# Transposing phi(k) and the attention output by DMA in a TensorE-bound attention + MLP kernel

## The chip, the cores, the metric

One core of one Trainium2 chip. The metric is the device time of one execution in microseconds (us), the median of several runs.

## The reference, cut to what matters

```python
xn = layernorm(x)                                  # x: 2048 x 1024
out = x + A(xn) + B(xn)

# A: 32 heads of 32, four segments of 512 tokens, one after the other
q, k, v = xn @ wq, xn @ wk, xn @ wv
phi(t) = where(t > 0, t + 1, exp(t))
for s in range(4):
    a_dot = softmax(q_s k_s^T * scale + mask) @ v_s          # inside the segment
    a_mem = (phi(q_s) @ M) / (phi(q_s) @ z + 1e-6)           # memory of earlier segments
    o_s   = g * a_mem + (1 - g) * a_dot
    M += phi(k_s)^T @ v_s ;  z += sum of phi(k_s)
A = o @ wo

# B: MLP over tokens: hidden 3584
B = (gelu(layernorm(xn)^T @ w1 + b1) @ w2 + b2)^T
```

The output of the memory update for the last segment is never used, so phi(k) is needed for three of the four segments only.

## The kernel before

After the norm and the first MLP product, the attention runs in 32 *units*: unit `u` is segment `s = u // 8` and group `g = u % 8` of four heads. The second MLP product and the product with `wo` (*main* matmuls below) are emitted in slices between the pieces of a unit, so that TensorE has work while ScalarE, VectorE and GpSimd make the softmax weights. `LEAD = 2`: the projections of q and k are made two units ahead.

Operands lie in SBUF; matmuls write into PSUM, which this kernel uses as banks 0 to 7. A result is *evacuated* when ScalarE or VectorE copies it from its bank to SBUF. Both operands that have to be transposed go through TensorE with an identity matrix, into PSUM, and back:

```python
def proj_k(self, u, b):                       # k^T of one unit: 128 (4 heads x 32) x 512 tokens
    ...  # 8 matmuls into bank b
    fw.op("dve", lambda e: e.tensor_copy(self.kT[k][:], self.bank(b)), ...)

def k_transpose(self, u, b):                  # tokens to the partitions, for M += phi(k)^T v
    bb = self.bank_bf(b)[:, 0:512]
    with fw.group(reads=[self.R_kT[k], self.R_ident], writes=[self.R_bank[b]]):
        for c in range(4):
            fw.tp(bb[:, c * P:(c + 1) * P], self.kT[k][:, c * P:(c + 1) * P], self.ident[:])
    fw.op("act", lambda e: e.activation(self.etmp[1][:], bb, ACT.Exp), ...)
    self.phi(self.pk[j][:]..., self.R_pk[j], bb, self.R_bank[b], 1)    # DVE: min, then add + max

def o_transpose(self, u, b):                  # output of a unit, for the product with wo
    ...  # four tp of o_s into bank b, then:
    fw.op("act", lambda e: e.activation(self.oT[s % 2][:, g, :], bb, ACT.Copy), ...)

def proj_v(self, m, c, b):
    ...  # 8 matmuls into bank b
    fw.op("dve", lambda e: e.tensor_copy(self.vA[i][:, c, :, 0:D_HEAD], ...), ...)

for u in range(N_UNIT):
    n = 28 if s == 0 else 36                  # main matmuls in this unit
    n0, n1, n2 = (10, 8, 6) if s == 0 else (11, 9, 9)
    n3 = n - n0 - n1 - n2
    self.logits(u, 0)                         # banks 0-3, then one Exp on ACT
    if u: self.combine(u - 1)                 # DVE: o_s of the unit before
    self.main_emit(n0)
    self.logits(u, 1); self.main_emit(n1)
    self.logits(u, 2); self.main_emit(n2)
    self.weigh(u, 0); self.weigh(u, 1)
    self.proj_q(un, 0)                        # un = u + 2
    if u: self.o_transpose(u - 1, 2)
    if ...: self.k_transpose(u + 1, 3)        # not for segment 3
    self.weigh(u, 2)
    self.proj_k(un, 1)
    self.weigh(u, 3)                          # the last one also updates M with pk
    if ...: self.proj_v(m, u % 4, 2)
    self.main_emit(n3)
```

A helper (`FW`) puts the semaphore waits in. One of its rules matters here: two engines that read the same PSUM bank wait for each other, so readers of one bank run one after the other.

The softmax here doesn't subtract the row's maximum and nothing guards it: scores larger than these inputs give would overflow.

## Time and profile before

| | kernel before |
|---|---|
| median | 758.41 us (fast runs 757.46 to 758.64) |
| profiled span | 756.9 us, clock 0.999 |
| TensorE (PE) busy | 717.7 us, 95% |
| one unit, segment 0 / segment 1 | 14.48 / 16.57 us |

The unit lengths are distances between the first logits matmuls of one unit and the next in the timeline of TensorE (means of units 1 to 6, and 9 to 14).

The page of the kernel before: busy time of each engine with its share of the span, and shares of the chain that ended last.

```profile
PE 717.7 (95%) x5058; PEld 338.3 (45%) x5154; DVE 277.2 (37%) x617; ACT 280.4 (37%) x301; POOL 112.3 (15%) x154
...
PE 92%; DVE 4%; issue 2%; SPq 1%; DMA 1%; ACT 0%; DVEq 0%; another core or an unknown queue 0%
```

The table of stretches of the same kernel; the columns are named in its head.

```profile
core 0: us, PE busy (x) PEld busy (x) DVE busy (x) ACT busy (x) POOL busy (x), PEclk, DMA share, GB/s
...
350.00:420.00 70.00, 68.56 (x565) 33.01 (x574) 35.74 (x79) 29.16 (x32) 10.90 (x16) 1.00 0.34 72
420.00:490.00 70.00, 68.59 (x539) 32.28 (x547) 36.92 (x79) 28.95 (x29) 11.21 (x16) 1.00 0.35 74
```

In the attention part TensorE has 68.6 us of work in every 70 us; VectorE and ScalarE are half as busy. So a microsecond counts only if it is one of TensorE's.

What the transposes cost on TensorE is read from *starts*. The timeline of the kernel before (start, duration, engine, line, operation, count), inside one unit of segment 1 (unit 14):

```profile
463.16 1.89 PE L188 MATMUL ps_all<-xnT_70,wq_666 128*128 128x512 bf16 x8
464.88 0.39 PE L194 MATMUL ps_all<-ident,o_s_1739 128*128 128x128 bf16 x4
465.10 0.39 PE L194 MATMUL ps_all<-ident,kT_1727 128*128 128x128 bf16 x4
465.33 0.46 PE L188 MATMUL ps_all<-vA_64,pT 128*128 128x33 bf16 x12
```

The records say 0.39 us for each group of four, but they overlap: the next group starts 0.22 us later, and the work after it 0.23 us later. A group of four transposes is worth about 0.22 us, not 0.39.

The same timeline where attention starts (in brackets the idle time before it, and what ended it):

```profile
237.57 0.39 PE L194 MATMUL ps_all<-ident,kT_1727 128*128 128x128 bf16 x4
239.70 0.40 PE L188 MATMUL ps_all<-qT_1724,kT_1727 32*128 32x512 bf16 x4 [1.74 <-DVE pk_1733 L673]
```

The first k transpose lies in bank 0, which the first logits need; TensorE waits until phi has read it.

### The profile page before, as it was taken

The numbers are of one execution on the slowest core, as the hardware profiler recorded it, in microseconds if no ns is written. First come the engines' busy times: TensorE is split into PE (matmuls) and PEld (weight loads), VectorE is DVE, ScalarE is ACT, GpSimd is POOL, SyncE is SP. The second block draws the span as 40 slices with busy tenths as digits, with TensorE's granted clock in tenths as the row PEclk, the third lists the DMA queues.
The fourth block names the chain that finished last, engine by engine and source line by source line (L and its number), as shares of the span: only waits on it lengthen the run. The fifth ranks groups of instructions, "written<-read, shape, count | busy, mean of one in ns | idle before, by whom it ended". The sixth has DMA issues, their size and how long they took to land.

```text
span 756.9 us, 11693 instructions
## 1 busy us (share of the span) xinstructions
PE 717.7 (95%) x5058; PEld 338.3 (45%) x5154; DVE 277.2 (37%) x617; ACT 280.4 (37%) x301; POOL 112.3 (15%) x154
## 2 busy tenths in 40 slices
PE   0999999999998999999999999999999999999996
PEld 0544444444443444444444444444444444444442
DVE  6920000000002343344444555544455553444443
ACT  2781212121213434435444434444443444343430
POOL 3630000000000111111121111112111111211220
PEclk9999999999999999999999999999999999999999
DMA  9439224225307161461542506054250615415003
GB/s 255 136 100 218 72 56 112 55 59 133 49 25 194 29 132 52 83 132 34 100 90 44 120 15 133 31 102 91 42 119 15 132 33 101 102 33 105 15 5 121
DMA packets 164604, 65.79 MB, mean 87 GB/s; under 512 B 125642, under 2 KB 156362, under 8 KB 164554
## 3 DMA queue, kind: packets, MB, share of 16 engines
q1 hardware_dynamic: 164554, 65.04, 36.8%
q8 instruction: 41, 0.67, 0.4%
q14 instruction: 9, 0.07, 0.0%
HBM read 59.79 MB, written 5.24 MB: 86 GB/s over the span
## 4 chain that ended last, share of the span: by engine, by line
PE 92%; DVE 4%; issue 2%; SPq 1%; DMA 1%; ACT 0%; DVEq 0%; another core or an unknown queue 0%
PE ps_all L188 90%; PE ps_all L194 2%; DVE ln_st L575 1%; SPq L210 1%; DVE ln_st L574 1%; DMA brow_51<-in_B_b_dram 1%; DVE ln_mv L576 0%; DVE xn_tmp_76 L607 0%; DVE ln_rs L584 0%; DVE fin_8202 L966 0%; DVE fin_8203 L966 0%; ACT xn_tmp_75 L604 0%; DVE xn_tmp_74 L607 0%; DVE ln_rs L585 0%; ACT xnT_70 L622 0%
## 5 line engine op out<-in xcount | busy, mean ns | idle before, releaser
L743 ACT ACTIVATE pT<-ps_all 128x1536 bf16<-128x1536 f32 (+1 forms) x96 | 152.9, 1593 | 201.6 <-PE ps_all L188 201.6
L749 POOL TENSOR_SCALAR_AFFINE_SELECT pT<-pT 128x512 bf16<-128x512 bf16 x128 | 86.9, 691 | 599.5 <-ACT pT L743 599.5
L662 ACT ACTIVATE gT<-ps_all,b1c 128x512 bf16<-128x512 f32 x56 | 37.8, 689 | 134.5 <-PE ps_all L188 134.5
L710 DVE CAST vA_63<-ps_all 128x512 bf16<-128x512 f32 x16 | 11.1, 694 | 187.9 <-PE ps_all L188 187.7
L188 PE MATMUL ps_all<-h,w1s_79 128*128 128x512 bf16 x311 | 72.9, 385 | 2.7 <-issue 2.2
L188 PE MATMUL ps_all<-h,w1s_80 128*128 128x512 bf16 x314 | 72.4, 381 | 0.3
L188 PE MATMUL ps_all<-h,w1s_81 128*128 128x512 bf16 x251 | 55.6, 379 | 0.3
L188 PE MATMUL ps_all<-gT,w2h_671 128*128 128x512 bf16 x213 | 53.0, 380 | 2.8 <-PE ps_all L188 0.9
L188 PE MATMUL ps_all<-gT,w2h_673 128*128 128x512 bf16 x214 | 53.1, 380 | 2.6 <-PE ps_all L188 1.1
L188 PE MATMUL ps_all<-gT,w2h_670 128*128 128x512 bf16 x219 | 53.6, 381 | 0.3
L188 PE MATMUL ps_all<-gT,w2h_672 128*128 128x512 bf16 x218 | 53.3, 381 | 0.4 <-PE ps_all L188 0.2
L783 DVE CAST ost_1736<-ps_all 128x264 bf16<-128x264 f32 (+1 forms) x64 | 23.7, 391 | 79.6 <-PE ps_all L188 79.6
L783 DVE CAST ost_1737<-ps_all 128x264 bf16<-128x264 f32 (+1 forms) x64 | 23.7, 392 | 74.7 <-PE ps_all L188 74.7
L188 PEld LDWEIGHTS ps_all<-h,w1s_80 128*128 128x128 bf16 x320 | 31.5, 98 | 38.4 <-issue 1.1
L188 PEld LDWEIGHTS ps_all<-h,w1s_79 128*128 128x128 bf16 x320 | 30.9, 99 | 37.1 <-issue 3.6
L188 PEld LDWEIGHTS ps_all<-h,w1s_81 128*128 128x128 bf16 x256 | 25.0, 98 | 30.2
L188 PE MATMUL ps_all<-wo_sb,oT_1744 128*128 128x512 bf16 x126 | 32.6, 380 | 1.4 <-remote 0.3
L188 PEld LDWEIGHTS ps_all<-gT,w2h_671 128*128 128x128 bf16 x224 | 19.4, 97 | 30.8 <-PE ps_all L188 6.9
L188 PEld LDWEIGHTS ps_all<-gT,w2h_673 128*128 128x128 bf16 x224 | 19.4, 97 | 30.8 <-PE ps_all L188 6.9
L188 PE MATMUL ps_all<-wo_sb,xnT_68 128*128 128x512 bf16 x127 | 30.6, 380 | 1.2 <-ACT xnT_68 L835 0.7
L188 PEld LDWEIGHTS ps_all<-gT,w2h_672 128*128 128x128 bf16 x224 | 19.3, 98 | 25.3 <-issue 3.6
L188 PEld LDWEIGHTS ps_all<-gT,w2h_670 128*128 128x128 bf16 x224 | 19.3, 98 | 25.3 <-issue 3.6
(167 smaller groups left out, 870.9 us busy)
## 6 DMA issues: line engine op xcount, KB each, us to landing
w1s_79<-in_B_w_dram SPq DMA_DIRECT2D x5, 1024.0 KB, 5.5
w1s_80<-in_B_w_dram SPq DMA_DIRECT2D x5, 1024.0 KB, 6.1
w1s_81<-in_B_w_dram SPq DMA_DIRECT2D x4, 1024.0 KB, 5.7
wq_666<-in_A_wq_dram SPq DMA_DIRECT2D x16, 256.0 KB, 3.2
wq_667<-in_A_wq_dram SPq DMA_DIRECT2D x16, 256.0 KB, 7.2
wk_668<-in_A_wk_dram SPq DMA_DIRECT2D x16, 256.0 KB, 2.9
wk_669<-in_A_wk_dram SPq DMA_DIRECT2D x16, 256.0 KB, 4.9
w2h_670<-in_B_w_dram SPq DMA_DIRECT2D x8, 448.0 KB, 4.8
```

Source lines behind the costliest of these rows:

```text
L188: ins = self.nc.tensor.matmul(*args, **kwargs)
L194: ins = self.nc.tensor.transpose(out, in_, ident)
L210: ins = es.eng.dma_start(out_ap, in_ap)
L574: fw.op("dve", lambda e: e.bn_stats(st[:, 0:6], src[:, 0:512]), reads=[self.R_xin[c]], writes=[R])
L575: fw.op("dve", lambda e: e.bn_stats(st[:, 6:12], src[:, 512:1024]), reads=[self.R_xin[c], R], writes=[R])
L662: fw.op("act", lambda e: e.activation(self.gT[:, fc, half * 512:(half + 1) * 512], self.bank(b), ACT.Gelu_apprx_tanh, bias=self.b1c[:, fc: ...
L710: fw.op("dve", lambda e: e.tensor_copy(self.vA[i][:, c, :, 0:D_HEAD], self.bank(b).rearrange("p (h d) -> p h d", d=D_HEAD)), reads=[self.R ...
L743: fw.op("act", lambda e: e.activation(self.pT[:, :, off:off + total], self.ps[:, 0:4, 0:total], ACT.Exp, scale=SCALE), reads=self.R_bank[0:4],
L749: fw.op("pool", lambda e: e.affine_select(d, d, pattern=[[0, 4], [1, P]], compare_op=ALU.is_ge, fill=0.0, base=0, channel_multiplier=-1), ...
L783: fw.op("dve", lambda e: e.tensor_copy(dst, self.ps[:, b, 0:n * VW]), reads=[self.R_bank[b]], writes=[self.R_ost[o][qb]])
```

## The change

The intent is to take 55 of the transposes (24 of phi(k), 31 of the output) off TensorE and let the DMA engines do them from SBUF to SBUF. phi(k) is now computed before the transpose, straight after the K projection: Exp reads the projection's bank. The first of k's transposes is issued straight after the projections of unit 0, no longer after those of unit 1. ScalarE, which loses the copies of the output, takes V's evacuation. V's product moves ahead of K's, and the fill counts `n0, n1, n2` change, so that more main matmuls stand between K's product and the next logits.

```diff
-        ins = es.eng.dma_start(out_ap, in_ap)
+        ins = es.eng.dma_start(out_ap, in_ap, transpose=True) if transpose else es.eng.dma_start(out_ap, in_ap)
...
 def proj_k
         fw.op("dve", lambda e: e.tensor_copy(self.kT[k][:], self.bank(b)), ...)
+        if u // N_GRP < N_SEG - 1:
+            fw.op("act", lambda e: e.activation(self.etmp[1][:], self.bank(b), ACT.Exp),
+                  reads=[self.R_bank[b]], writes=[self.R_etmp[1]])
+            self.phi(self.mtmp[1][:], self.R_mtmp[1], self.kT[k][:], self.R_kT[k], 1)
 def proj_v
-        fw.op("dve", lambda e: e.tensor_copy(self.vA[i]..., self.bank(b)...
+        fw.op("act", lambda e: e.activation(self.vA[i]..., self.bank(b)..., ACT.Copy),
-    def k_transpose(self, u, b):            # four tp, Exp, phi
...
+    def k_transpose(self, u):
+        j = u % 2
+        self.fw.dma(self.pk[j][:], self.mtmp[1][:], reads=[self.R_mtmp[1]], writes=[self.R_pk[j]], transpose=True)
+    def o_transpose_dma(self, u):
+        self.fw.dma(self.oT[s % 2][:, g, :]..., self.o_s[o][:]..., ..., transpose=True)
 loop over units
-            n0, n1, n2 = (10, 8, 6) if s == 0 else (11, 9, 9)
+            n0, n1, n2 = (9, 7, 6) if s == 0 else (10, 8, 8)
             self.logits(u, 2)
+            if u + 1 < N_UNIT and (u + 1) // N_GRP < N_SEG - 1:
+                self.k_transpose(u + 1)
+            if u:
+                self.o_transpose_dma(u - 1)
             self.main_emit(n2)
 ...
-            if u:
-                self.o_transpose(u - 1, 2)
-            if u + 1 < N_UNIT and (u + 1) // N_GRP < N_SEG - 1:
-                self.k_transpose(u + 1, 3)
             self.weigh(u, 2)
-            if un < N_UNIT:
-                self.proj_k(un, 1)
-            self.weigh(u, 3)
             m = u // 4 + 1
             if m < 2 * N_SEG:
                 self.proj_v(m, u % 4, 2)
+            self.weigh(u, 3)
+            if un < N_UNIT:
+                self.proj_k(un, 1)
             self.main_emit(n3)
```

The last output transpose, in the tail, stays on TensorE.

More of the change, by code (lines that the diff above doesn't have):

```diff
@@ L199, in dma @@
     def dma(self, out_ap, in_ap, reads=(), writes=(), is_output=False, issuer="sp", extra=(),
-            record_reads=True):
+            record_reads=True, transpose=False):
         es = self.E[issuer]
@@ L709, in proj_v @@
                       self.wv_sb[:, dc, bv * 512:(bv + 1) * 512], start=(dc == 0), stop=(dc == N_DCH - 1))
-        fw.op("dve", lambda e: e.tensor_copy(self.vA[i][:, c, :, 0:D_HEAD],
-                                             self.bank(b).rearrange("p (h d) -> p h d", d=D_HEAD)),
+        fw.op("act", lambda e: e.activation(self.vA[i][:, c, :, 0:D_HEAD],
+                                            self.bank(b).rearrange("p (h d) -> p h d", d=D_HEAD), ACT.Copy),
               reads=[self.R_bank[b]], writes=[self.R_vA[i][c]])
-    def k_transpose(self, u, b):
-        fw = self.fw
-        k, j = u % 3, u % 2
-        bb = self.bank_bf(b)[:, 0:512]
-        with fw.group(reads=[self.R_kT[k], self.R_ident], writes=[self.R_bank[b]]):
-            for c in range(4):
-                fw.tp(bb[:, c * P:(c + 1) * P], self.kT[k][:, c * P:(c + 1) * P], self.ident[:])
-        fw.op("act", lambda e: e.activation(self.etmp[1][:], bb, ACT.Exp),
-              reads=[self.R_bank[b]], writes=[self.R_etmp[1]])
-        self.phi(self.pk[j][:].rearrange("p c d -> p (c d)"), self.R_pk[j], bb, self.R_bank[b], 1)
+    def k_transpose(self, u):
+        j = u % 2
+        self.fw.dma(self.pk[j][:], self.mtmp[1][:], reads=[self.R_mtmp[1]], writes=[self.R_pk[j]], transpose=True)
     LOGIT_STEPS = [[0], [1], [2, 3]]
@@ L826, in combine @@
               reads=[self.R_prod], writes=[R_os])
+    def o_transpose_dma(self, u):
+        s, g, o = u // N_GRP, u % N_GRP, u % 2
+        self.fw.dma(self.oT[s % 2][:, g, :].rearrange("p (q t) -> p q t", q=4),
+                    self.o_s[o][:].rearrange("p q j -> p (q j)"),
+                    reads=[self.R_os[o]], writes=[self.R_oT[s % 2][g]], transpose=True)
     def o_transpose(self, u, b):
@@ L900, in attention_and_out @@
             self.proj_k(u, 6 + u)
-        self.k_transpose(0, 0)
+            if u == 0:
+                self.k_transpose(0)
         for u in range(N_UNIT):
```

## The prediction

> **What bounds the kernel.** TensorE. On the page PE is 95% busy and the chain that ended last is 92% PE. In the stretches table each 70 us between 280 and 700 us holds 68.4 to 69.0 us of PE work at full clock; DVE is about 50% busy, ACT 41%, DMA 0.34 to 0.42. Only what changes PE's own stream, or makes it wait, counts.
>
> **Removed from PE.** 31 transposes of the attention output and 24 of k, four 128x128 matmuls each. In the timeline of one unit (16.53 us) they start at 464.88 and 465.10, the next work at 465.33: 0.225 us per group, all on the critical path. 55 x 0.225 = 12.4 us. Other matmuls only change order.
>
> **Start of attention.** The timeline shows PE idle 1.74 us at 238 us, until phi(k) of unit 0 releases bank 0. That goes, but Exp of the second k now precedes the first logits Exp on ACT: net -1 us.
>
> **Moved.** V's cast (694 ns x28) leaves DVE; on ACT it replaces the copy of the output transposes (603 ns x31). Neither engine bounds: no direct gain. A unit now ends with K projection, main matmuls, next logits, which need K's bank. Its readers run one after the other (kT cast 0.68, Exp 0.6), about 1.4 us with hand-over. In segments 1 to 3 ten main matmuls (2.2 us) cover that; in segment 0 only six (1.3 us, counted from slightly earlier): 0.3 x 8 = +2.4 us. Shorter fill before the second logits, and waits for DMA semaphores: +1.
>
> **The DMA transposes.** 55 of 128 KB on the SP queue, up to two per unit. k's has about 10 us before the next DVE phi overwrites its source; the output's about 9 us before fused matmuls need it, and only in a segment's first unit. The Trainium skill (VectorE: DVE Perf Modes, "The three transpose paths") gives 1309 ns for a 128x128 DMA transpose; my estimate from it is at most 4 x 1.3 = 5.2 us, likelier 3, as fixed latency is not paid four times. Loads of 256 KB land in 3 to 7 us here (DMA table). Then nothing waits, and DMA's share rises from 0.37 to about 0.5. No trace here shows a DMA transpose: the weak point.
>
> **Sum.** 758.6 - 12.4 - 1 + 2.4 + 1 = 748.6; freed DVE may give a little back: 748 us, range 744 to 762. Faster by over 2% (below 743.5) 0.07, within 2% 0.77, slower 0.16.
>
> **What would show each step right.** In attention PE transposes only in the tail (4); a unit with both transposes 16.1 instead of 16.53 us in segments 1 and 2; in segment 0 about 14.3 instead of 14.45, with small PE gaps before its first logits, ended by ACT's Exp of k; the gap at 238 us gone; transposes landing in 2 to 6 us; no wait of PE on one; little DVE wait for the k product's buffer.
>
> **What would make it wrong.** Transposes that take 8 us or more each, or keep the SP queue or all DMA engines busy: then DVE stalls on the k product's buffer, everything behind it comes late, weight loads queued behind them land late, and PE waits in every unit; 24 units times several us would be slower by over 2%. If transposes took 2 us and segment 0's gap did not appear, the time would be 744 to 745.

## The result, and the profile after

The changed kernel took 747.72 us (747.44 to 748.58), against 758.41 us. The ratio is 0.9865, 95% interval 0.9846 to 0.9884. Ratios here and below are the mean time of one kernel's runs over that of the other's of the same rounds, so they are not quite the ratio of the medians. Executions over 1.5% slower than the fastest of the same kernel are left out of the means.

The page of the changed kernel, the same two lines:

```profile
PE 706.4 (95%) x4842; PEld 326.3 (44%) x4934; DVE 260.0 (35%) x585; ACT 286.6 (38%) x302; POOL 113.9 (15%) x154
...
PE 89%; DVE 5%; issue 2%; ACT 2%; SPq 1%; DMA 1%; DVEq 0%; ACTq 0%
```

The stretches of the changed kernel:

```profile
350.00:420.00 70.00, 68.40 (x516) 31.03 (x523) 34.96 (x75) 30.72 (x30) 11.48 (x17) 1.00 0.42 92
420.00:490.00 70.00, 68.45 (x532) 31.40 (x540) 33.65 (x72) 31.15 (x30) 13.60 (x20) 1.00 0.49 105
```

TensorE is still the limit, with the same density of work; DMA's share rose from about 0.35 to 0.42 to 0.49 here. The timeline of the same unit 14 in the changed kernel shows nothing between the Q projection and the products with V:

```profile
456.86 1.89 PE L188 MATMUL ps_all<-xnT_70,wq_666 128*128 128x512 bf16 x8
458.58 0.46 PE L188 MATMUL ps_all<-vA_64,pT 128*128 128x33 bf16 x12
458.89 0.22 PE L188 MATMUL ps_all<-MZbf,pqT_1732 128*128 128x132 bf16 x1
458.94 1.89 PE L188 MATMUL ps_all<-wv_sb,xnT_70 128*128 128x512 bf16 x8
```

The start of attention in the changed kernel (TensorE and ScalarE): the wait of 1.74 us is gone, but a new one of 1.04 us follows. Exp of the second k (L703) runs first on ScalarE, so the Exp of the first logits (L740) starts only at 238.06, and the next logits need the banks that it reads.

```profile
236.50 0.40 PE L188 MATMUL ps_all<-qT_1724,kT_1727 32*128 32x512 bf16 x4
236.83 2.12 PE L188 MATMUL ps_all<-gT,w2h_670 128*128 128x512 bf16 x9
237.57 0.60 ACT L703 ACTIVATE etmp_1741<-ps_all 128x512 bf16<-128x512 f32 x1 [1.26 <-DVE kT_1728 L700]
238.06 1.87 ACT L740 ACTIVATE pT<-ps_all 128x2048 bf16<-128x2048 f32 x1
239.99 0.34 PE L188 MATMUL ps_all<-qT_1724,kT_1727 32*128 32x384 bf16 x4 [1.04 <-ACT pT L740]
```

At the end of each unit of segment 0 the first logits of the next unit are late. This is the timeline of TensorE, VectorE and ScalarE at the end of unit 1 in the changed kernel (lines of other instructions left out):

```profile
263.12 1.67 PE L188 MATMUL ps_all<-xnT_68,wk_669 128*128 128x512 bf16 x7
...
264.63 1.46 PE L188 MATMUL ps_all<-gT,w2h_671 128*128 128x512 bf16 x6
264.83 0.69 DVE L700 CAST kT_1727<-ps_all 128x512 bf16<-128x512 f32 x1 [0.90 <-PE ps_all L188]
265.61 0.60 ACT L703 ACTIVATE etmp_1741<-ps_all 128x512 bf16<-128x512 f32 x1 [2.55 <-DVE kT_1727 L700]
...
266.35 0.40 PE L188 MATMUL ps_all<-qT_1726,kT_1729 32*128 32x512 bf16 x4 [0.27 <-ACT etmp_1741 L703]
```

Cast, then Exp, then the bank is free: 1.4 us from 264.83 to 266.2, and only six main matmuls to cover it. The gap of 0.27 us is there eight times, before the first logits of units 1 to 8.

The transposes in the DMA table of the changed kernel (tiles, issuing queue, count, median us from issue to landing; the output goes to `oT` in segments 0 and 2, to `xnT_68` in 1 and 3):

```profile
pk_1733<-mtmp_1743 SPq DMA_TRANSPOSE x12, 2.4
pk_1734<-mtmp_1743 SPq DMA_TRANSPOSE x12, 6.0
oT_1744<-o_s_1738 SPq DMA_TRANSPOSE x8, 2.3
oT_1744<-o_s_1739 SPq DMA_TRANSPOSE x8, 3.8
xnT_68<-o_s_1738 SPq DMA_TRANSPOSE x8, 2.3
xnT_68<-o_s_1739 SPq DMA_TRANSPOSE x7, 2.8
```

Where the 10.80 us between the two profiled spans lie, from starts in the two timelines of TensorE:

| stretch | before | after | difference |
|---|---|---|---|
| up to the first Q projection | 230.66 | 229.50 | -1.16 |
| Q projection to the first logits | 9.04 | 7.00 | -2.04 |
| unit 0 | 14.29 | 15.52 | +1.23 |
| units 1 to 7 (segment 0) | 101.33 | 100.58 | -0.75 |
| units 8 to 22 | 248.69 | 242.05 | -6.64 |
| units 23 to 30 | 120.84 | 119.34 | -1.50 |
| unit 31 and tail | 32.05 | 32.11 | +0.06 |

The first row is not the change's: nothing is different there but who evacuates V, and over the 13 profiles this point lies anywhere from 229.38 to 230.92 us. About 9.6 us are the change's own. A second series of the changed kernel, beside other runs, gave 748.62 us against 758.50 us, that is 9.9 us.

### The profile page after: what moved, and what is told of

Read it like the earlier page. It is cut to its first block, busy times and chain, and to the rows that moved or that the text cites. A ratio compares the mean times of both kernels' runs of the same rounds, so it can differ in the third digit from the quotient of the medians.

```text
span 746.1 us, 11381 instructions
## 1 busy us (share of the span) xinstructions
PE 706.4 (95%) x4842; PEld 326.3 (44%) x4934; DVE 260.0 (35%) x585; ACT 286.6 (38%) x302; POOL 113.9 (15%) x154
## 3 DMA queue, kind: packets, MB, share of 16 engines
q1 hardware_dynamic: 194474, 72.26, 42.8%
## 4 chain that ended last, share of the span: by engine, by line
PE 89%; DVE 5%; issue 2%; ACT 2%; SPq 1%; DMA 1%; DVEq 0%; ACTq 0%
PE ps_all L188 89%; DVE ln_st L575 1%; SPq L210 1%; DVE ln_st L574 1%; DMA brow_51<-in_B_b_dram 1%; ACT etmp_1741 L703 1%; DVE kT_1727 L700 0%; DVE ln_mv L576 0%; PE ps_all L194 0%; DVE kT_1729 L700 0%; DVE kT_1728 L700 0%; ACT pT L740 0%; DVE xn_tmp_76 L607 0%; ACT L703 0%; DVE fin_8047 L970 0%
## 5 line engine op out<-in xcount | busy, mean ns | idle before, releaser
L740 ACT ACTIVATE pT<-ps_all 128x1536 bf16<-128x1536 f32 (+1 forms) x96 | 152.9, 1593 | 111.0 <-PE ps_all L188 111.0
L746 POOL TENSOR_SCALAR_AFFINE_SELECT pT<-pT 128x512 bf16<-128x512 bf16 x128 | 88.4, 703 | 587.8 <-ACT pT L740 587.8
L700 DVE CAST kT_1727<-ps_all 128x512 bf16<-128x512 f32 x11 | 7.6, 690 | 198.5 <-PE ps_all L188 198.5
L188 PE MATMUL ps_all<-gT,w2h_673 128*128 128x512 bf16 x211 | 55.0, 380 | 2.7 <-PE ps_all L188 0.5
L188 PE MATMUL ps_all<-gT,w2h_671 128*128 128x512 bf16 x211 | 54.5, 380 | 3.1 <-PE ps_all L188 1.1
L188 PE MATMUL ps_all<-gT,w2h_672 128*128 128x512 bf16 x220 | 53.7, 381 | 0.2
L188 PE MATMUL ps_all<-gT,w2h_670 128*128 128x512 bf16 x221 | 53.6, 381 | 0.3 <-PE ps_all L188 0.2
L703 ACT ACTIVATE etmp_1741<-ps_all 128x512 bf16<-128x512 f32 x24 | 14.3, 597 | 58.1 <-DVE kT_1729 L700 20.7
L188 PEld LDWEIGHTS ps_all<-gT,w2h_671 128*128 128x128 bf16 x224 | 19.4, 97 | 30.8 <-PE ps_all L188 6.9
L188 PEld LDWEIGHTS ps_all<-gT,w2h_673 128*128 128x128 bf16 x224 | 19.3, 97 | 30.3 <-PE ps_all L188 6.9
L188 PE MATMUL ps_all<-wo_sb,oT_1744 128*128 128x512 bf16 x127 | 30.3, 380 | 1.2
L188 PE MATMUL ps_all<-wo_sb,xnT_68 128*128 128x512 bf16 x127 | 29.3, 379 | 1.4 <-ACT xnT_68 L838 0.8
L188 PEld LDWEIGHTS ps_all<-gT,w2h_670 128*128 128x128 bf16 x224 | 19.3, 98 | 25.3 <-issue 3.8
```

What stands on the lines that cost most here:

```text
L188: ins = self.nc.tensor.matmul(*args, **kwargs)
L703: fw.op("act", lambda e: e.activation(self.etmp[1][:], self.bank(b), ACT.Exp), reads=[self.R_bank[b]], writes=[self.R_etmp[1]])
L740: fw.op("act", lambda e: e.activation(self.pT[:, :, off:off + total], self.ps[:, 0:4, 0:total], ACT.Exp, scale=SCALE), reads=self.R_bank[0:4],
L746: fw.op("pool", lambda e: e.affine_select(d, d, pattern=[[0, 4], [1, P]], compare_op=ALU.is_ge, fill=0.0, base=0, channel_multiplier=-1), ...
```

## The experiments

All outputs are right. Unit lengths are read from the TensorE timeline as above.

### Neither transpose by DMA: the order alone

```diff
 the changed kernel, with
+ k_transpose on TensorE (bank 3), Exp and phi of k after it, as in the kernel before
+ o_transpose on TensorE (bank 1, as bank 2 now holds V's product)
```

> The changed kernel with both transposes back on TensorE; V evacuated by ACT, V's product ahead of K's, and the new fill counts stay. Theory (only the 55 transposes taken off TensorE count, 12.4 us): the time is that of the kernel before, 758 us, within 1.5 us; no PE gap before the logits of segment 0. Rival (the order and the relief of DVE give part of the 10.7 us): 756 us or less.

Measured: 760.13 us, before 758.53 us in the same rounds, ratio 1.0022 (1.0005 to 1.0039). That is 1.6 us slower than the kernel before, just outside what was expected, but the cause is an edit of this experiment: in units 28 and 29 V has no product any more, so K's product follows closely on the output's transpose in the same bank 1. The timeline of this kernel shows it, and once more at 711.07 us with 0.92:

```profile
694.70 0.22 PE L188 MATMUL ps_all<-MZbf,pqT 128*128 128x132 bf16 x1
695.84 1.46 PE L188 MATMUL ps_all<-xnT,wk 128*128 128x512 bf16 x6 [0.93 <-ACT xnT L845]
```

These two units are 0.87 and 0.86 us longer than before, together 1.7 us, which is the whole difference. All other units are as long as in the kernel before (14.48 and 16.57 us). So V's move to ScalarE, the new order and the new fill counts give no gain by themselves.

### Only k, only the output

```diff
 k_only: the changed kernel, with o_transpose on TensorE (bank 1)
 o_only: the changed kernel, with k_transpose on TensorE (bank 3) and its Exp and phi after it
```

> Only phi(k) is transposed by DMA; the output's 31 transposes are back on TensorE. Theory: 31 x 0.225 = 7.0 us slower than the changed kernel, about 754.7 us, with the gaps of 0.27 us before the logits of segment 0 still there. Rival (DMA transposes of the output cost something by contention that cancels part of their gain): less than 5 us slower than the changed kernel.

> Only the output is transposed by DMA; k's 24 transposes are back on TensorE, and Exp reads the transposed k in PSUM as before. Theory: +5.4 us for the transposes, -2.2 us because the 8 gaps of 0.27 us in segment 0 go, about +0.7 us at the start of attention: near 751.6 us, 4 us slower than the changed kernel. Rival (k's DMA transposes disturb the weight loads on the same queue): 749 us or less.

Measured: k only 757.07 us (ratio 0.9981, 0.9967 to 0.9996), output only 752.01 us (0.9914, 0.9899 to 0.9928), before 758.53 us. k only has the same two gaps of 0.93 and 0.92 us as the run above; less some 1.7 us for them it would be at 755.4 us, near the 754.7 expected. The units tell it more cleanly (units 1 to 6 and 9 to 14):

| | segment 0 | segment 1 |
|---|---|---|
| before; neither | 14.48 | 16.57 |
| k by DMA only | 14.60 | 16.35 |
| output by DMA only | 14.26 | 16.35 |
| both (the changed kernel) | 14.37 | 16.12 |

In segment 1 each of the two is worth 0.22 to 0.23 us per unit, and they add up to 0.45. That is the spacing of one group of four in the timeline of the kernel before. In segment 0 the output's is worth 0.22 again, but k's costs 0.11 to 0.12: it saves 0.22 and brings a wait of about 0.33. Both rivals fall: nothing is lost to contention in a unit.

### V's evacuation back on VectorE

```diff
-        fw.op("act", lambda e: e.activation(self.vA[i]..., self.bank(b)..., ACT.Copy),
+        fw.op("dve", lambda e: e.tensor_copy(self.vA[i]..., self.bank(b)...),
```

> The changed kernel with V's evacuation back on DVE. Theory (DVE and ACT both have slack, so it does not matter who does it): within 0.5 us of the changed kernel, 747.7 us. Rival (moving V's cast to ACT was needed to keep DVE ahead of K's cast): 2 us or more slower, with PE gaps before the logits that end with the cast of k.

Measured: 748.76 us, ratio 0.9872 (0.9858 to 0.9887). That is 1.0 us over the 747.72 expected, but the changed kernel itself came out at 748.62 us in a later series, and the units are the same to 0.01 us (14.38, 16.12). The gaps are the same too. In the profiles the two kernels differ by 0.9 us, of which 0.85 lie before the first Q projection (230.35 against 229.50). From there to the end both take 516.6 to 516.7 us, so who evacuates V does not matter there.

### K's product first again

```diff
-            (V's product; weigh(u, 3); K's product)
+            (K's product; weigh(u, 3); V's product)
```

> The changed kernel with the old order: K's product before V's. Theory (the 0.27 us gaps of segment 0 come from K's bank being read by the cast and then by Exp with only six main matmuls to cover it): V's product covers it, the 8 gaps go, 2.2 us faster than the changed kernel, about 745.5 us. V's bank has one reader of 0.6 us, covered by six matmuls. Rival (the order does not matter, the gap only moves to V's bank): within 0.7 us of the changed kernel.

Measured: 746.18 us (745.5 expected), ratio 0.9846 (0.9829 to 0.9862). Units of segment 0 fell from 14.37 to 14.04 us, those of segment 1 stayed at 16.12. The gaps before the first logits are gone. The new order, meant to make room, cost segment 0 about 0.33 us per unit: behind V's product six matmuls are enough, as V's bank has one reader; behind K's they are not.

### Exp of k from the SBUF copy

```diff
-            fw.op("act", lambda e: e.activation(self.etmp[1][:], self.bank(b), ACT.Exp),
-                  reads=[self.R_bank[b]], writes=[self.R_etmp[1]])
+            fw.op("act", lambda e: e.activation(self.etmp[1][:], self.kT[k][:], ACT.Exp),
+                  reads=[self.R_kT[k]], writes=[self.R_etmp[1]])
```

> The changed kernel, but Exp of k reads the bf16 copy of k in SBUF, not the PSUM bank; the bank is free after the cast. Theory: the 0.27 us gaps of segment 0 go, 8 x 0.27 = 2.2 us faster, about 745.5 us. Rival (something else held PE there, ACT being late for the first logits): no gain, the gap stays with another name.

Measured: 745.52 us, ratio 0.9839 (0.9824 to 0.9854). The timeline of this kernel at the end of unit 1, to be held against the one above:

```profile
264.64 1.46 PE L188 MATMUL ps_all<-gT,w2h 128*128 128x512 bf16 x6
264.84 0.69 DVE L700 CAST kT<-ps_all 128x512 bf16<-128x512 f32 x1 [0.90 <-PE ps_all L188]
265.56 0.63 ACT L703 ACTIVATE etmp<-kT 128x512 bf16<-128x512 bf16 x1 [2.49 <-DVE kT L700]
266.02 0.10 PEld L188 LDWEIGHTS ps_all<-qT,kT 32*128 32x128 bf16 x4 [0.42 <-DVE kT L700]
266.03 0.40 PE L188 MATMUL ps_all<-qT,kT 32*128 32x512 bf16 x4
```

Exp runs at the same time as before, but the logits no longer wait for it; they start at 266.03, not 266.35. Two different edits, this and the one above, take the same 0.33 us off each unit of segment 0. The cause of the gap is shown: two readers of K's bank in a row, with six matmuls of cover.

### Every transpose twice

```diff
-            if ...: self.k_transpose(u + 1)
-            if u: self.o_transpose_dma(u - 1)
+            for _ in range(2):
+                if ...: self.k_transpose(u + 1)
+            for _ in range(2):
+                if u: self.o_transpose_dma(u - 1)
```

The second waits for the first to land, as it writes the same place. (96 DMA semaphores in place of 64, so that none is reused too early.)

> The changed kernel with every DMA transpose but the first issued twice, into the same place. Theory (the transposes have 9 to 10 us of slack and land in 2 to 6 us, so they are off the critical path): within 1 us of the changed kernel, while DMA's share of the 16 engines rises from 0.43 to about 0.49. Rival (transposes slow the loads behind them on the queue and already cost something): 3 us or more slower, with PE waiting for w2 or DVE for the k product's buffer.

Measured: 753.24 us (750.79 to 753.89), ratio 0.9930 (0.9911 to 0.9950). The expectation was wrong: 5.5 us slower than 747.72, 4.6 us than the later series. The rival had the size right (3 us or more), but not the cause: in the profile TensorE never waits for w2, and VectorE only once for a transpose of k (2.0 us; 1.9 in the changed kernel). The profiled run was the fastest one, 750.79 us. In it DMA's queue took 46.8% of the 16 engines (42.8% in the changed kernel), all units are as long as before but two, and TensorE waited twice for a transpose: 2.56 us in unit 8, shown here, and 0.77 us in unit 16:

```profile
366.16 0.60 PE L188 MATMUL ps_all<-gT,w2h 128*128 128x512 bf16 x2
369.32 1.89 PE L188 MATMUL ps_all<-wo_sb,oT 128*128 128x512 bf16 x8 [2.56 <-DMA oT<-o_s]
```

These are the first units of a segment, where the main matmuls read the outputs of the segment before, the last of which was transposed a moment ago. The slack there is smaller than predicted. The SP queue of the *changed* kernel in unit 8:

```profile
355.07 0.47 SPq L210 DMA_DIRECT2D w2h_672<-in_B_w_dram  x1
355.58 0.81 SPq L210 DMA_DIRECT2D w2h_673<-in_B_w_dram  x1
356.43 3.61 SPq L210 DMA_TRANSPOSE pk_1734<-mtmp_1743  x1
360.09 1.26 SPq L210 DMA_TRANSPOSE oT_1744<-o_s_1739  x1
```

The issue of k's transpose takes 3.61 us behind two loads of w2 (1.19 us is the shortest of all), and the output's has to wait for it. It landed 2.7 us after 360.09, at 362.8, and TensorE read it at 367.01. From issue to need that is 6.9 us, where the prediction had about 9; after the landing 4.2 us of slack are left. In the doubled kernel the two k transposes hold the queue for 6.76 us, and the output's start at 363.48.

### Every transpose twice, the output's first

> The kernel with every transpose doubled, but the two of the output issued ahead of the two of k. In the doubled kernel before it, 753.2 us, the profile showed PE waiting for the output's transpose only in the first unit of a segment (2.56 and 0.77 us). If that deadline is the whole cost of doubling: PE waits at most 0.5 us for it, and the time falls to 747.5 to 749 us, although the DMA work is the same. Rival (the doubled DMA work itself slows the weight loads): it stays at 751 us or more.

Measured: 749.27 us, 0.3 above the stated 747.5 to 749, ratio 0.9881 (0.9864 to 0.9897), and the changed kernel in the same rounds 748.62 us. The DMA queue took 47.1% of the engines, as much as in the run above, but no wait of TensorE for a transpose is left. So the doubled work itself costs 0.65 us at most, and by the profiles less: from the first Q projection to the end the reordered kernel takes 516.68 us and the changed kernel 516.66. The rest of the loss, 4 us, came from the order on the queue. (The doubled kernel ran in another series; the kernel before took 758.30 us there and 758.50 here.) In the profiled run of the doubled kernel the two late units hold all of it, 3.0 us. Its runs at 753 us were not profiled; that their further 2.5 us lie in the same two units is not shown. The reordered kernel has no runs of that kind.

The swap also shows what makes an issue long. In unit 8 of the reordered kernel the two transposes of the output, now right behind the w2 loads, hold the queue for 6.98 us and the two of k behind them for 4.16. In the doubled kernel it was k's two for 6.76 and the output's for 4.49. It is so in all units: a pair directly behind a w2 load holds the queue for 6.4 to 8.8 us, whether it is k's or the output's (one of 5.87 apart), and a pair elsewhere mostly for 3.5 to 5.7. The place behind the loads counts, not the tile. VectorE now waits eleven times for k's transposes, 27.5 us in all, and TensorE loses nothing by it.

### Three mends, and a fourth

```diff
 combined: Exp of k from the SBUF copy, as above, and
+        k_phi(1), split from proj_k(1), emitted after the three logits of unit 0
+        weigh(u, 1); main_emit(3); weigh(u, 2)     # only for the last two units, which project nothing
 combined_tail: and
-            if b == 3: self.o_transpose(u, 3)       # the tail's transpose, in the bank of the next group
+            if b == 5: self.o_transpose(u, 3)       # one group of seven matmuls earlier
```

> The changed kernel with three mends: Exp of k from the SBUF copy; Exp and phi of unit 1 put behind the logits of unit 0, so that ACT's first logits Exp does not wait (1.04 us of PE gap at 240 us); three main matmuls between the second and third product of the last two units, where PE waited 0.36 us twice for DVE. Theory: 2.2 + 1.0 + 0.7 = 3.9 us faster than the changed kernel, about 743.8 us. If only the first mend works: 745.5 us.

> The combined kernel with the last output transpose, which stays on TensorE in the tail, moved one group of seven matmuls earlier, so that the matmuls of another bank cover ACT's copy. Theory: the PE gap of 0.78 us in the tail goes, 744.1 becomes 743.4 us. Rival (the gap moves to another bank or to the output DMAs): no change.

Measured: combined 744.14 us, ratio 0.9818 (0.9803 to 0.9832), with 745.52 us for the first mend alone in the same rounds. Unit 0 took 14.43 us (14.98 with the first mend alone, 15.52 in the changed kernel): the gap of 1.04 us (0.84 with the first mend alone) went, and one of 0.20 us came at VectorE's copy of a result. The two gaps of 0.36 us in the last units went. With the tail's mend: 743.66 us, ratio 0.9805 (0.9790 to 0.9819), beside the changed kernel's 748.62 us in the same rounds (0.9871, 0.9857 to 0.9886). The tail's gap of 0.78 us, the same in the changed kernel, is no longer in the timeline.

> The changed kernel once more, in the same rounds as the two others, so that they have it beside them: 747.7 us within 0.7 us.

Measured: 748.62 us (748.59 to 748.87), 0.9 us above the first series and a little outside the expected 0.7. A difference of 1 us in time between series is therefore nothing to build on. The profiles say where it lies: 0.69 us of the 0.71 between the two profiles of the changed kernel come before the first Q projection (229.50 and 230.19). From there to the end they take 516.64 and 516.66 us, and the kernel before 526.27. Kernels that differ only in the attention are best compared over that stretch: there the change is worth 9.6 us in both profiles.

## Why the prediction was right

It said 748 us, 744 to 762, "within 2%" most likely; measured were 747.72 and 748.62 us. The mechanism held, and the large terms with it; that the small ones add up is partly luck.

- **TensorE bounds, only its stream counts.** Right. The order and V's move alone gave nothing; moving V back changed no unit. So the 0.6 us that the prediction took off for a freed VectorE have nothing behind them.
- **55 groups at 0.225 us, 12.4 us.** Right. Each kind measured 0.22 to 0.23 us per unit in segment 1, and the units with both fell from 16.57 to 16.12 us (predicted 16.1). Reading the spacing of starts, not the durations of records, made this come out: with the 0.39 us of a group's record the sum would have been 21 us.
- **Start of attention, net -1 us.** -0.81 measured (-2.04 and +1.23 in the table). These two rows also hold two of the 55 groups (-0.45) and the first of the eight waits of the next point (+0.33); without them about -0.7 is left. The mechanism is as told: the wait for bank 0 went, and the second k's Exp delayed the first logits' Exp.
- **Segment 0, 0.3 us per unit, +2.4.** Right: the gaps show 0.27 us, and the two edits that remove them take 0.33 us per unit, about 2.6 us for eight. Units of segment 0 were predicted at 14.3 and measured 14.37 us.
- **+1 us for shorter fill and semaphore waits.** No such wait appears in the units. What took its place was not predicted: a gap of 0.36 us in each of the last two units, where the output's transpose had covered VectorE's copy. Unit 30 therefore gained nothing (11.26 us before and after). That the sum came out in spite of this term is luck.
- **The DMA transposes.** Off the critical path, as said. The Trainium skill (VectorE: DVE Perf Modes, "The three transpose paths") gives 1309 ns for a 128x128 transpose by DMA; the estimate of 5.2 us at most and likelier 3 for a 128x512 one is met by five of the six medians (2.3 to 3.8 us), not by the sixth. That one, 6.0 us, is for every second transpose of k, and all twelve of these follow a w2 load directly on the queue. DMA's share rose to 0.43, less than the 0.5 told: the 54 transposes that the doubled kernel adds take 0.6 us of all 16 engines each ((0.468 x 749.1 - 0.428 x 746.1) / 54); by the same sum the first 55, from the kernel before to the changed one, take 0.7. Wrong in size: the output's time from issue to need in a segment's first unit, 6.9 us in unit 8 in place of about 9, with 4.2 us left after the landing. Its data was ready at 355.26 (the end of VectorE's last instruction on it); what the prediction does not name is that k's transpose stands before it on the same queue and itself comes behind loads, so that it was issued at 360.09 only. It did not matter here; doubled, it cost about 4 us.
- The small part of the gain in the profile that lies before the first Q projection (1.16 us) was neither predicted nor made by the change; it varies from run to run.

## What to carry to other kernels

When one engine bounds, count what a change takes off it by the distance of starts in its timeline, and then look at each place where the removed work had covered something: a bank with two readers in a row, or the last units without projections. Here such waits kept back some 4 of the 12 us, and small edits won them back (748.62 to 743.66 us; a little of that is the tail's gap, which was there before the change too, with 0.69 us). Work moved to the DMA engines needs a look at its deadline *and* at what stands before it on the issuing queue: order transfers by how soon they are needed.

## What the Trainium skill lacked or had wrong

- TensorE: Matmul & The Clock Gate, "Part 4: PE-mode transpose", gives about 390 ns for a 128x128 bf16 transpose alone and about 275 ns in one kernel. Here each record is 219 ns, but four in a row take only 0.22 us of TensorE's time, some 56 ns each, and removing them gains just that. Part 4 lacks the spacing of transposes in a row (other parts of the page treat that of plain matmuls), and it decides whether a DMA transpose is worth it.
- VectorE: DVE Perf Modes, "The three transpose paths", has one figure for the DMA, 1309 ns for 128x128. It lacks that a 128x512 transpose from SBUF to SBUF lands in 2.3 to 2.4 us (medians) where no load of w2 stands just before it on the queue, and in 6.0 us (median) for `pk_1734`, right behind such loads.
- DMA: Bandwidth & Descriptors has no time for how long a transpose occupies the issuing queue on this chip (it has cycle counts of "previous generations", beside those of a later chip, without naming this one). Here it was 1.19 us at the shortest, against 0.58 us for a load of 256 KB, and 3.5 us (median) and up to 4.7 us for every second transpose of k (pk_1734), as in unit 8 behind two w2 loads; what is queued next waits that long.
- Advanced Engine Details and Errata, "X-Bar Transpose (TRN2)", says that transpose DMAs are as fast as regular ones. The trace roughly agrees in the time of the DMA engines per byte, taken from differences of the queue's totals. The 54 added transposes of the doubled kernel moved 7.1 MB in 31 us of all 16 engines (227 GB/s), the 55 of the change 7.2 MB in 41 us (177 GB/s), and everything that the kernel before moved on this queue 65.0 MB in 279 us (233 GB/s). It does not agree in time to landing (2.3 us for 128 KB, and only 2.6 to 3.9 for most loads of twice the size) or in the time of issue (previous point).
